# Moving the first sub-block's row moves ahead of a weight load, that load's cast to VectorE, and two pairs of band builds two units earlier, and dropping a gate on `w_out`

## The chip, the cores and the metric

The kernel runs on one core of one Trainium2 chip. The metric is device time in microseconds (us) of that core for one execution; lower is better. A run "of the same rounds" is a run of the kernel before that was taken on the same chip, in turn with the kernel it is compared with.

## The reference

A dynamic convolution over seven positions (weights from a softmax) feeds a feed-forward layer with squared ReLU:

```python
w = exp(weight_gen - max); w = w / sum(w)                # 8 x 4096 x 8 heads x 7
out = einsum('bshk,bskhg->bshg', w, windows of padded x) # x: 8 x 4096 x 192
x = out.reshape(32768, 192)
h = maximum(x @ w_in, 0)                                 # w_in: 192 x 2048
return h * h @ w_out                                     # w_out: 2048 x 192
```

## The kernel before

The work is cut into 64 sub-blocks of 512 tokens; blocks 0 and 1 have one sub-block, all others two. In each block, TensorE does three kinds of work. The convolution is a multiplication of x with band matrices. The *units* multiply with `w_in` (16 of them in a block of two sub-blocks; ScalarE applies the ReLU and VectorE squares, giving `g`). The *output matmuls* multiply `g` with `w_out`.

The convolution needs bands, which VectorE builds from the softmax weights. In the first sub-blocks, the rows of these weights are moved from one place in SBUF to another by small DMAs ("row moves", tile `wr`):

```python
def st_band(j, tiles):            # cut: one multiplication of moved rows with a mask
    nc.vector.tensor_tensor(out=bd_t[j][...], in0=wr_t[j][...], in1=mask[...], op=AluOp.mult)
```

The start of the program, with cuts:

```python
spin(25)                                  # warm-up matmuls on zeros
s0.load(nc.sync); s1.load(nc.sync)        # weight_gen of the first two parts
load_w_in(w_st[0], 0, nc.sync)            # first half of w_in, 768 KB as float32
x_load_f32(0)
load_w_in(w_st[1], 1, nc.sync)            # second half
# ... softmax of s0 and s1: exp on ScalarE, the rest on VectorE ...
nc.scalar.copy(out=w_i[:, 0, 0], in_=w_st[0])
wr_load_sbuf(0, [s0], range(NT), (nc.gpsimd,))   # row moves, sub-block 0
wr_load_sbuf(1, [s0], range(NT), (nc.sync,))
x_cast(0, nc.scalar.copy)
cross_w_in_by_pe(0)     # other partition half of w_in, first half: through TensorE
spin(14)
x_load_f32(1)
nc.scalar.copy(out=w_i[:, 1, 0], in_=w_st[1])
cross_w_in(1)           # the same for the second half: two 192 KB DMAs ("crossed copy")
# ... row moves of sub-blocks 2 and 3 ...
for i in range(NT):
    st_band(0, (i,))
st_conv(0)
nc.gpsimd.tensor_copy(out=gate, in_=x_st[1][:, 0:1])  # GpSimd waits for x here
for q in range(4):
    load_w_out(q, 4)
```

The output matmuls of most blocks use two PSUM banks, each with half of the contraction. ScalarE copies the first bank, then VectorE adds the second one, and only then is the pair free for the next output matmuls:

```python
def o_sum(j, qt, ccs, o):
    ...
    nc.scalar.copy(out=o_sb, in_=o[0][:, c])
    if len(o) == 2:
        nc.vector.tensor_tensor(out=o_sb, in0=o[1][:, c], in1=o_sb, op=AluOp.add)
```

A table places the bands of the next block at two units of the current one. Block 5 is made of sub-blocks 8 and 9, so block 4 builds their bands:

```python
us = {4: (10, 12), 6: (7, 9)}.get(j, (5, 9) if small else (1, 5))
for n, u in enumerate(us):
    at(j, u, "B", a + n)
```

The softmax here doesn't subtract the row's maximum and nothing guards it: scores larger than these inputs give would overflow.

Of the kernel before, what the change touches and what calls it, by code (L numbers as in the profile page):

```python
# [9 lines left out]
def kernel(  # L10
# [26 lines left out]
    nc = tc.nc  # L37
    f32 = mybir.dt.float32
# [9 lines left out]
    P = 128  # L48
# [13 lines left out]
    NT = 5  # L62
# [9 lines left out]
    const = ctx.enter_context(tc.tile_pool(name="const", bufs=1))  # L72
# [17 lines left out]
    w_i = const.tile([P, WQ, 2, NQ + NQ // 2], f16, name="w_i")  # L90
# [32 lines left out]
    x_st = {}  # L123

    def load_w_in(dst, q, eng):
        c = q * NQ
        eng.dma_start(out=dst[:, 0:NQ], in_=moe_w_in[0:P, c : c + NQ])  # L127
        for r0 in (0, RT):
            eng.dma_start(  # L129
                out=dst[r0 : r0 + RT, NQ:], in_=moe_w_in[P:D, c : c + NQ // 2]  # L130
            )
            c += NQ // 2

    def cross_w_in(q):
        for r0, r1 in ((0, RT), (RT, 0)):
            nc.sync.dma_start(out=w_i[r0 : r0 + RT, q, 1], in_=w_i[r1 : r1 + RT, q, 0])
# [144 lines left out]
    def tile_start(j, i):  # L281

        t1 = (j % NBB + 1) * TB
        return TB - P if i == NT - 1 and t1 in ends(j // NBB) else starts[i]
# [21 lines left out]
    def x_load_f32(j):  # L306
        x_st[j] = p_one.tile([P, (R + HALO) * HK], f32, name="x_st", tag="ex")
        block_load(
            j, x_st[j][:, 0 : NT * D].rearrange("p (t d) -> p t d", t=NT), x[j // NBB], D, nc.sync
        )  # L310

    def x_cast(j, copy):
        x_t[j] = p_x.tile([P, NT, D], f16, name="xt")
        copy(out=x_t[j].rearrange("p t d -> p (t d)"), in_=x_st[j][:, 0 : NT * D])
# [6 lines left out]
    def wr_load_sbuf(j, parts, order, engines):  # L321

        wr_t[j] = p_wr.tile([P, NT, HP, SL * 2], f16, name="wr")
        n = 0
        for i in order:
            t0 = max(j % NBB * TB + tile_start(j, i), 0)
            for s in parts:
                a, b = max(t0, s.t0), min(t0 + P, s.t0 + P * s.r)
                if a < b:
                    engines[n % len(engines)].dma_start(  # L330
                        out=wr_t[j][a - t0 : b - t0, i].rearrange("p g c -> p (g c)"),
                        in_=s.v[
                            (a - s.t0) // s.r : (b - s.t0) // s.r, HALO : HALO + s.r
                        ].rearrange("p r g c e -> p r (g c e)"),
                    )
                    n += 1

    def st_band(j, tiles):


        if j not in bd_t:
            bd_t[j] = p_bd.tile([P, H * NT * STEP], f16, name="bd")
        i = tiles[0]
        lo = STEP * i
        shift = 0 if i == 0 and j % NBB == 0 else lo - tile_start(j, i)
        n = min(STEP, P - shift)
        shape = (P, HP * len(tiles), n // SL, 2 * SL)
        nc.vector.tensor_tensor(  # L348
            out=bd_t[j][:, H * lo : H * (lo + len(tiles) * n)].rearrange(
                "p (g m c) -> p g m c", g=shape[1], c=2 * SL  # L350
            ),
            in0=wr_t[j][:, i : tiles[-1] + 1]
            .rearrange("p t g c -> p (t g) c")
            .unsqueeze(2)
            .broadcast_to(shape),
            in1=mask[:, shift : shift + n]
            .rearrange("p (m c) e -> p m (c e)", c=SL)
            .unsqueeze(1)
            .broadcast_to(shape),
            op=AluOp.mult,  # L360
        )
# [8 lines left out]
    def conv_pieces(j):  # L370


        s0, n = BLOCKS[j]
        th = n * TB // 2
        halves = []
        for half in (0, 1):
            s, a = (s0 + half, 0) if n == 2 else (s0, th * half)
            halves.append([
                (s, i, half, max(bounds[i], a), min(bounds[i + 1], a + th), a)
                for i in range(NT) if bounds[i] < a + th and bounds[i + 1] > a  # L380
            ])
        if n == 2:
            for k in range(NK):
                for later in (True, False):
                    for pair in zip(*halves):
                        for s, i, half, a, b, base in pair:
                            for q in (2 * k, 2 * k + 1):
                                yield later, s, i, q, half, a, b, base
        else:
            for pair in zip(*halves):  # L390
                for later in (True, False):
                    for k in range(NK):
                        for s, i, half, a, b, base in pair:
                            for q in (2 * k, 2 * k + 1):
                                yield later, s, i, q, half, a, b, base

    def st_conv(j):

        n = BLOCKS[j][1]
        th = n * TB // 2  # L400
        per = 1024 // th
        y = p_y.tile([P, NK, TB], f16, name="y")
        y_t[j] = y
        yps = [
            ps_h.tile([P, 2 * TB], f32, name="yp", tag="h") for _ in range(-(-NK // per))
        ]
        for later, s, i, q, half, a, b, base in conv_pieces(j):
            lo = bounds[i]
            hi = lo + (STEP if tile_start(s, i) == starts[i] else bounds[i + 1] - lo)
            _, ha, hb, pre = quads[q]  # L410
            m, h = (32, hb) if later else (pre, ha)
            bd = bd_t[s][:, H * lo : H * hi].rearrange("p (g c e) -> p g e c", g=HP, e=2)
            p0 = RT * half + 32 * (q % 2)
            k = q // 2
            col = th * (k % per) - base
            nc.tensor.matmul(  # L416
                out=yps[k // per][p0 : p0 + m, col + a : col + b],
                lhsT=x_t[s][:, i, 32 * q : 32 * q + m],
                rhs=bd[:, h // 2, h % 2, a - lo : b - lo],
                start=True,  # L420
                stop=True,
                skip_group_check=True,
                tile_position=(0, p0),
            )
        for n, yp in enumerate(yps):
            k0, k1 = n * per, min((n + 1) * per, NK)
            nc.scalar.copy(  # L427
                out=y[:, k0:k1, 0:th],
                in_=yp[:, 0 : (k1 - k0) * th].rearrange("p (k c) -> p k c", c=th),
            )  # L430
# [79 lines left out]
    with nc.allow_low_precision("fp16 matmul pipeline"), tc.manual_schedule():  # L510
# [16 lines left out]
                wr_load_sbuf(j, near, range(NT), engines)  # L527

        warm = const.tile([P, TB], f16, name="warm")
        gate = const.tile([P, 1], f32, name="gate")  # L530
        nc.vector.memset(warm, 0.0)  # L531
        for v in v_first:
            nc.vector.memset(v, 0.0)
# [3 lines left out]
        def spin(n):  # L537
# [3 lines left out]
        s0, s1, s2 = parts[:3]  # L541
# [6 lines left out]
        w_st = [  # L548
            p_wg.tile([P, (R + HALO) * HK], f32, name="w_st", tag="wg")[:, 0 : NQ + NQ // 2]
            for q in (0, 1)  # L550
        ]
        load_w_in(w_st[0], 0, nc.sync)
        x_load_f32(0)
        load_w_in(w_st[1], 1, nc.sync)
        for s in (s0, s1):
            s.exp(0, s.rh)
            s.total(0, s.rh)
            s.recip(0, s.rh)
            s.scale(0, s.rh, nc.vector)
        nc.scalar.copy(out=w_i[:, 0, 0], in_=w_st[0])  # L560
        wr_load_sbuf(0, [s0], range(NT), (nc.gpsimd,))
        wr_load_sbuf(1, [s0], range(NT), (nc.sync,))
        x_cast(0, nc.scalar.copy)
        cross_w_in_by_pe(0)
        spin(14)
        x_load_f32(1)
        nc.scalar.copy(out=w_i[:, 1, 0], in_=w_st[1])
        cross_w_in(1)
        wr_load_sbuf(2, [s0, s1], range(NT), (nc.gpsimd,))
        wr_load_sbuf(3, [s0, s1], range(NT), (nc.sync,))  # L570
        for i in range(NT):
            st_band(0, (i,))
        st_conv(0)

        nc.gpsimd.tensor_copy(out=gate, in_=x_st[1][:, 0:1])
        for q in range(4):
            load_w_out(q, 4)
        s2.load(nc.gpsimd)
# [18 lines left out]
        def at(j, u, kind, *args):  # L597
            fill.setdefault((j, u), []).append((kind, *args))
# [34 lines left out]
        for j in range(len(plans), NBLK - 1):  # L633
            a = BLOCKS[j + 1][0]
            small = [p for p in parts if p.fb <= j + 1][-1].r == FIRST
            us = {4: (10, 12), 6: (7, 9)}.get(j, (5, 9) if small else (1, 5))
            for n, u in enumerate(us):
                at(j, u, "B", a + n)
        for j in range(len(plans), NBLK):
# [86 lines left out]
        j = NBLK - 1  # L726
# [44 lines left out]
```

## Time and profile before

| | us |
|---|---|
| median of three runs | 750.5 (750.27 to 751.14) |
| span of the profiled run | 749.5 |
| TensorE busy | 739.9 |
| first convolution starts | 16.45 |
| first unit starts | 18.41 |
| crossed copy has landed | 19.0 |
| first output matmuls start | 24.56 |
| conv of block 5, start to start with the next work | 2.43 (1.53 for block 4's) |

Lines of the timeline have the start, the length, the engine, the line in the source, the operation, the tiles as out<-in, the shapes and the count. A bracket at the end gives the idle time of that engine just before, and what ended it. A group of several instructions may contain short gaps. TensorE is the bound throughout (busy 739.9 of 749.5 us): a change gains only by shortening the few stretches in which TensorE stands. The prediction shows the profile lines and reads them.

### The profile page before, as it was taken

To read this page: it belongs to the slowest core of one execution; us is meant where nothing else is said; L and a number is where in the kernel's file an instruction comes from. 1 tells how busy PE (TensorE), PEld (TensorE's weight loads), DVE (VectorE), ACT (ScalarE), POOL (GpSimd) and SP (SyncE) were. 2 spreads that over 40 slices of the span, in tenths; PEclk is the share of its full clock that TensorE was granted. 3 is DMA by queue.
4 is the path that set the end of the run, shared out by engine and by line. 5 is a ranking of instruction groups with operands and counts; after the bars stand their busy time and mean duration, and the time that the engine had idled before them with its cause. 6 is when DMAs were issued, how large, how long until landed. Compare 5 with 4: busy or idle time off the path is not lost.

```text
span 749.5 us, 33282 instructions
## 1 busy us (share of the span) xinstructions
PE 739.9 (99%) x15106; PEld 567.9 (76%) x15106; DVE 622.4 (83%) x1001; ACT 624.3 (83%) x755; POOL 89.4 (12%) x129
## 2 busy tenths in 40 slices
PE   7999999999999999999999999999999999999998
PEld 3867778877887777777877887787777777777787
DVE  6898898998889888888888888898888987677853
ACT  4998978888888888888888888888888887888883
POOL 7222220001101000011000110001100011000000
PEclk9999999999999999999999999999999999999999
DMA  7745444445453244543245442365441354342312
GB/s 216 117 97 117 79 67 114 99 76 138 94 116 64 76 73 80 128 90 66 45 80 138 87 80 53 51 138 108 59 80 46 58 108 80 59 72 52 50 45 65
DMA packets 122398, 64.81 MB, mean 86 GB/s; under 512 B 84107, under 2 KB 118865, under 8 KB 121745
## 3 DMA queue, kind: packets, MB, share of 16 engines
q1 hardware_dynamic: 77969, 45.69, 22.5%
q0 software_dynamic: 44144, 16.90, 20.1%
q8 instruction: 118, 1.93, 1.0%
q14 instruction: 23, 0.19, 0.1%
q10 hardware_dynamic: 144, 0.10, 0.0%
HBM read 48.61 MB, written 28.70 MB: 103 GB/s over the span
## 4 chain that ended last, share of the span: by engine, by line
PE 95%; DVE 2%; ACT 1%; DMA 1%; issue 0%; SPq 0%; ACTq 0%; DVEq 0%
PE o L475 45%; PE h L441 44%; PE yp L416 6%; DMA w_st<-in_moe_w_in_dram 1%; DVE bd L348 1%; DVE g L453 1%; ACT t L450 1%; PE wp L539 1%; DVE o_sb L491 0%; ACT w_i L560 0%; ACT y L427 0%; PE pt L144 0%; SPq L195 0%; SPq L129 0%; SPq L127 0%
## 5 line engine op out<-in xcount | busy, mean ns | idle before, releaser
L450 ACT ACTIVATE t<-h 128x1024 f16<-128x1024 f32 x512 | 496.7, 1027 | 66.7 <-PE h L441 66.1
L453 DVE TENSOR_TENSOR g<-t 128x1024 f16<-128x1024 f16 x512 | 335.5, 689 | 104.9 <-ACT t L450 102.7
L475 PEld LDWEIGHTS <-g 64*128 64x128 f16 (+1 forms) x8032 | 355.5, 94 | 51.7 <-issue 5.2
L475 PE MATMUL o<-w_o,g 64*128 64x192 f16 (+1 forms) x8032 | 387.3, 243 | 0.7 <-issue 0.5
L441 PE MATMUL h<-y,w_i 64*128 64x512 f16 (+1 forms) x3168 | 380.7, 370 | 1.4 <-ACT y L427 1.0
L441 PEld LDWEIGHTS <-w_i 64*128 64x128 f16 x3168 | 172.4, 94 | 108.2 <-issue 3.8
L348 DVE TENSOR_TENSOR bd<-wr,mask 128x4160 f16<-128x4160 f16 (+3 forms) x89 | 149.4, 1703 | 2.4 <-DMA wr<-v_first 2.3
L300 POOL DMA_DIRECT2D xt<-in_x_dram x62 | 51.7, 836 | 434.2 <-PE yp L416 411.1
L489 ACT COPY o_sb<-o 128x384 f32<-128x384 f32 x129 | 62.3, 483 | 32.9 <-PE o L475 32.9
L491 DVE TENSOR_TENSOR o_sb<-o,o_sb 128x384 f32<-128x384 f32 x123 | 68.4, 556 | 7.8 <-ACT o_sb L489 5.6
L427 ACT CAST y<-yp 128x1024 f16<-128x1024 f32 (+1 forms) x64 | 48.1, 802 | 15.9 <-PE yp L416 15.8
L416 PE MATMUL yp<-bd,xt 128*32 128x104 f16 (+8 forms) x3864 | 51.5, 208 | 0.6 <-DVE bd L348 0.4
L416 PEld LDWEIGHTS <-xt 128*32 128x32 f16 (+3 forms) x3864 | 46.0, 92 | 7.0 <-issue 6.7
L217 ACT ACTIVATE ex<-wg 128x448 f32<-128x448 f32 (+2 forms) x44 | 27.1, 615 | 2.2 <-DMA wg<-in_weight_gen_dram 2.2
L239 DVE TENSOR_TENSOR v_big<-ex,rcp 128x112 f16<-128x112 f32 (+1 forms) x136 | 27.4, 265 | 1.6 <-DMA vd<-v_big 0.4
L224 DVE TENSOR_REDUCE ssum<-ex 128x64 f32<-128x448 f32 (+2 forms) x44 | 26.2, 596 | 2.4 <-ACT ex L217 2.4
L231 DVE RECIPROCAL rcp<-ssum 128x64 f32<-128x64 f32 (+2 forms) x44 | 23.7, 539 | 1.5
L330 POOL DMA_DIRECT2D wr<-v_first x30 | 16.3, 562 | 34.4 <-DVE v_first L239 33.2
L290 POOL DMA_DIRECT2D xt<-in_x_dram x7 | 3.8, 549 | 133.1 <-PE yp L416 133.1
L539 PE MATMUL wp<-warm 128*128 128x512 f16 x39 | 12.3, 488 | 1.3 <-DVE warm L531 1.3
L539 PEld LDWEIGHTS <-warm 128*128 128x128 f16 x39 | 4.6, 119 | 8.3 <-issue 4.7
L239 DVE TENSOR_TENSOR v_first<-ex,rcp 128x112 f16<-128x112 f32 (+1 forms) x48 | 9.1, 257 | 0.3
(24 smaller groups left out, 29.1 us busy)
## 6 DMA issues: line engine op xcount, KB each, us to landing
out_dram<-o_sb SPq DMA_DIRECT2D x63, 384.0 KB, 2.9
xt<-in_x_dram POOLq DMA_DIRECT2D x42, 240.0 KB, 6.2
wg<-in_weight_gen_dram SPq DMA_DIRECT2D x4, 1064.0 KB, 7.9
xt<-in_x_dram POOLq DMA_DIRECT2D x20, 192.0 KB, 5.5
wr<-vd SPq DMA_DIRECT2D x38, 80.0 KB, 3.7
vd<-v_big SPq DMA_DIRECT2D x5, 512.0 KB, 5.7
wg<-in_weight_gen_dram SPq DMA_DIRECT2D x5, 392.0 KB, 5.2
wg<-in_weight_gen_dram SPq DMA_DIRECT2D x3, 616.0 KB, 5.2
```

The costliest lines, as they stand in the source:

```text
L217: nc.scalar.activation(out=self.ex[:, lo:hi].rearrange("p r g k e -> p (r g) k e"), in_=self.wg[:, lo:hi].rearrange("p r (g e) k -> p (r g ...
L239: eng.tensor_tensor(out=bass.AP(tensor=v.tensor, offset=v.offset + lo * H * SL + lo % SL * 2 + g * SL * 2, ap=[list(v.ap[0]), [H * SL + 2, ...
L300: eng.dma_start(out=dst[:, first:last], in_=ap)
L348: nc.vector.tensor_tensor(out=bd_t[j][:, H * lo : H * (lo + len(tiles) * n)].rearrange("p (g m c) -> p g m c", g=shape[1], c=2 * SL), in0= ...
L416: nc.tensor.matmul(out=yps[k // per][p0 : p0 + m, col + a : col + b], lhsT=x_t[s][:, i, 32 * q : 32 * q + m], rhs=bd[:, h // 2, h % 2, a - ...
L427: nc.scalar.copy(out=y[:, k0:k1, 0:th], in_=yp[:, 0 : (k1 - k0) * th].rearrange("p (k c) -> p k c", c=th),)
L441: nc.tensor.matmul(out=h[:, half, jj * th : (jj + 1) * th], lhsT=w_in_chunk(u * per + jj, slot, half), rhs=y_t[j][r0 : r0 + RT, k, 0:th], ...
L450: nc.scalar.activation(out=t1, in_=h, func=ActF.Relu)
L453: nc.vector.tensor_tensor(out=g, in0=t1, in1=t1, op=AluOp.mult)
L475: nc.tensor.matmul(out=oo[:, cc * Dm : (cc + 1) * Dm], lhsT=g[r0 : r0 + n, cc * P : (cc + 1) * P], rhs=w_o[r0 : r0 + n, fc, :], start=(fc ...
L489: nc.scalar.copy(out=o_sb, in_=o[0][:, c])
L491: nc.vector.tensor_tensor(out=o_sb, in0=o[1][:, c], in1=o_sb, op=AluOp.add)
```

## The change

The intent has three parts. The row moves of sub-block 0 are issued ahead of the second half of `w_in`, so that the first bands come earlier; in before that half was issued from 4.56 us and the moves from 8.63 us, and VectorE's wait for the moves ended at 13.90 us, 0.2 us after ScalarE's wait for the half. That half is then late and VectorE casts it, since it would follow the bands anyway. `w_out` no longer waits behind a GpSimd copy that reads x (1.13 us, after a wait of 1.55 us for that x). Far from the start, the bands for block 5 are placed two units earlier, so its convolution need not wait for them.

```diff
-        gate = const.tile([P, 1], f32, name="gate")
 ...
         load_w_in(w_st[0], 0, nc.sync)
         x_load_f32(0)
-        load_w_in(w_st[1], 1, nc.sync)
 ...
         nc.scalar.copy(out=w_i[:, 0, 0], in_=w_st[0])
-        wr_load_sbuf(0, [s0], range(NT), (nc.gpsimd,))
-        wr_load_sbuf(1, [s0], range(NT), (nc.sync,))
+
+        wr_load_sbuf(0, [s0], range(NT), (nc.sync, nc.gpsimd, nc.sync, nc.gpsimd, nc.gpsimd))
+        load_w_in(w_st[1], 1, nc.sync)
+        wr_load_sbuf(1, [s0], range(NT), (nc.gpsimd,))
         x_cast(0, nc.scalar.copy)
         cross_w_in_by_pe(0)
         spin(14)
         x_load_f32(1)
-        nc.scalar.copy(out=w_i[:, 1, 0], in_=w_st[1])
-        cross_w_in(1)
         wr_load_sbuf(2, [s0, s1], range(NT), (nc.gpsimd,))
-        wr_load_sbuf(3, [s0, s1], range(NT), (nc.sync,))
         for i in range(NT):
             st_band(0, (i,))
+        nc.vector.tensor_copy(out=w_i[:, 1, 0], in_=w_st[1])
+        cross_w_in(1)
+        wr_load_sbuf(3, [s0, s1], range(NT), (nc.sync,))
         st_conv(0)
-
-        nc.gpsimd.tensor_copy(out=gate, in_=x_st[1][:, 0:1])
         for q in range(4):
 ...
-            us = {4: (10, 12), 6: (7, 9)}.get(j, (5, 9) if small else (1, 5))
+            us = {4: (8, 10), 6: (7, 9)}.get(j, (5, 9) if small else (1, 5))
```

## The prediction

> **What bounds the kernel now.** I read the page first: busy shares, then the chain that ended last.
>
> ```profile
> PE 739.9 (99%) x15106; PEld 567.9 (76%) x15106; DVE 622.4 (83%) x1001; ACT 624.3 (83%) x755; POOL 89.4 (12%) x129
> ...
> PE 95%; DVE 2%; ACT 1%; DMA 1%; issue 0%; SPq 0%; ACTq 0%; DVEq 0%
> ```
>
> TensorE is busy 739.9 of 749.5 us and is 95% of the chain. So whatever the change does can act on the time in two ways only: it removes or adds time in which TensorE stands, or it does nothing. There are about 10 us in which TensorE stands, and all three parts of the change together can win a share of those. Next I read the chain in order of time for the first 20 us, because two of the three parts act there.
>
> ```profile
> 9.49 1.48 ACT w_i L560
> ...
> 11.82 4.71 PE wp L539 x14
> 16.52 1.02 PE yp L416 x55
> ```
>
> Columns: start, length, what. After the cast of the first w_in half, the chain runs through the 14 warm-up matmuls (L539) and then into the first convolution (L416), which starts at 16.5 us. The timeline of the same stretch shows what else is ready at 16.5 us:
>
> ```profile
> 8.63 4.45 POOL L330 DMA_DIRECT2D wr<-v_first  x8 [1.64 <-DVE v_first L239]
> ...
> 10.12 1.46 DVE L239 TENSOR_TENSOR v_first<-ex,rcp 128x112 f16<-128x112 f32 x8
> ...
> 13.68 1.47 ACT L567 CAST w_i<-w_st 128x1536 f16<-128x1536 f32 x1 [0.43 <-DMA w_st<-in_moe_w_in_dram]
> 13.90 4.87 DVE L348 TENSOR_TENSOR bd<-wr,mask 128x832 f16<-128x832 f16 x7 [2.32 <-DMA wr<-v_first]
> ```
>
> The row moves are issued from 8.63 us, but VectorE stands 2.32 us until the first of them has landed, at 13.90 us, 5.2 us after its issue (the view of tile wr gives 1.9 / 4.2 / 5.2 us from issue to landing as least, median and most). The second w_in half ends ScalarE's wait at 13.68 us, 0.2 us before. So the small moves landed right behind that 768 KB load (one 512 KB and two 128 KB issues). Five bands of one sub-block then take 13.90 to 16.50 us (0.50 us apart). **Two things are therefore ready at the same moment: the bands at 16.50 and the warm-up matmuls at 16.52.** Removing one alone frees nothing. The clock by stretches shows how long the warm-up lasts and why:
>
> ```profile
> 8.48:11.90 3.42, 1.10 (x6) 0.41 (x5) 3.03 (x10) 2.41 (x3) 3.27 (x6) 1.00 1.03 303
> 11.90:15.31 3.41, 3.41 (x10) 1.17 (x9) 1.41 (x3) 2.82 (x3) 2.41 (x6) 0.50 0.51 100
> ```
>
> First columns: stretch, length, TensorE busy; then weight loads, VectorE, ScalarE and GpSimd; the last three are granted clock, DMA share and GB/s. TensorE was busy 1.10 of 3.42 us (it stood 2.31 us for the first w_in half), and in the next stretch its clock was 0.50. DMA was full (1.03) until 11.9 us.
>
> Far from the start I looked for places where TensorE stands. The timeline of VectorE and of TensorE around 91 to 105 us, block 4, shows the largest:
>
> ```profile
> 93.56 0.69 DVE L453 TENSOR_TENSOR g<-t 128x1024 f16<-128x1024 f16 x1 [0.22 <-ACT t L450]
> 94.17 0.55 DVE L491 TENSOR_TENSOR o_sb<-o,o_sb 128x384 f32<-128x384 f32 x1
> 94.64 2.38 DVE L348 TENSOR_TENSOR bd<-wr,mask 128x832 f16<-128x832 f16 x2
> ...
> 98.14 2.35 DVE L348 TENSOR_TENSOR bd<-wr,mask 128x3328 f16<-128x3328 f16 x2
> ```
>
> ```profile
> 94.59 1.66 PE L475 MATMUL o<-w_o,g 64*128 64x192 f16 x32
> ...
> 100.08 1.86 PE L416 MATMUL yp<-bd,xt 128*32 128x104 f16 x118 [0.41 <-DVE bd L348]
> ```
>
> The convolution of block 5 begins at 99.44 and waits for its second pair of bands (ends 100.50). Start to start it takes 99.44 to 101.87 = 2.43 us, against 76.64 to 78.17 = 1.53 us for the one before: 0.90 us lost. The output matmuls at 102.53 take 1.55 instead of 1.33 us, waiting for a late sum on VectorE: 0.22 us more.
>
> [...]
>
> **The change, part by part.**
>
> *Moves ahead of the second half.* The moves of sub-block 0 now stand behind the first half and x only (ScalarE starts to cast that x at 10.87). Estimate from the least landing times of the same tile (1.9 to 2.8 us): issued 8.63 to about 10.4, landed by about 11 to 12.7. VectorE finishes both softmaxes at 11.58. So its bands run 11.6 to about 14.2 (5 x 0.50 plus a tail) instead of 13.9 to 16.5: **2.3 us earlier**. What that gives depends on the warm-up, whose count the diff leaves at 14:
> - Clock at 0.50 as in this profile: warm-up still ends at 16.5. Gain 0.
> - Clock full: 14 matmuls take 14 x 0.217 = 3.0 us from 11.65, so they end at 14.7. Before, bands hid that; now the convolution starts at 14.7. Gain 1.8 us.
>
> [...] I give the full clock 55%. Expected gain 1.0 us.
>
> *The second half later, cast by VectorE.* It is issued about 10.1 to 11.9 instead of 4.56 to 6.5. DMA engines then have only it, so I estimate landing at 14.5 to 15. The cast of 1536 columns is about 1.41 us (VectorE's 960-column cast, L314, took 0.88; x 1.6), and ends near 16.3; sub-block 1's bands (2.35) end near 18.7 and the cast of x near 19.6, as now (19.57). The crossed copy leaves at 16.3 instead of 15.2 and lands 3.3 to 3.8 us later (median 3.3), by 20.1. The first unit that needs it starts about 22.2 (20.4 in the fast case). Off the path, with little margin in the fast case. ScalarE loses a 1.47 us cast after which it stood idle anyway (2.4 us until L427): nothing.
>
> *w_out not held back.* Without the gate copy (1.13 us and a 1.55 us wait for x) GpSimd goes on after its moves. It has 14 of them now instead of 11, at about 0.55 us, so they end near 16.3 and w_out starts 2.0 us earlier (18.30 now). No TensorE wait for w_out is in the list of waits, so alone it gives nothing; in the fast case it is needed, since the first output matmuls move up to about 22.8 us.
>
> *Bands of block 5 at units 8 and 10.* The 0.90 and 0.22 us above should go. But VectorE keeps program order, and the first pair now stands before the g of units 8 and 9 and before the sum at 94.17, which frees the second output bank. The pair costs 96.94 - 94.64 = 2.30 us start to start. It can start at 92.53; the two g follow at 94.83 and 95.43 (0.60 each), the sum at 96.03, and ends near 96.58 instead of 94.72. The slack used up is 0.43 us. The output matmuls at 94.59 need that bank (they are already 0.11 us longer than 1.33), so **TensorE stands 1.87 us at 94.7**. Net: 1.87 - 0.90 - 0.22 = +0.75 us. TensorE is the bound from there to the end, so this stays.
>
> Sum: 750.5 - 1.0 + 0.75 = 750.25, taken as 750.2.
>
> **Rivals.**
> - *Full gain at the start in every run* (the warm-up no longer holds): for it, the two ends differed by 0.02 us only. Against it, the warm-up is unchanged and stands in the chain. Then 749.4.
> - *Half clock in most runs:* nothing won at the start, 751.25.
> - *The new stand at 94.7 trips the clock.* [...] I give it 10%.
> - *The output bank does not hold TensorE:* the last change alone gains 1.1 us. Against it, the matmul at 94.59 already waits for this very sum. Then 748.4 to 749.4.
> - *The second half is late:* TensorE waits at unit 4 for the crossed copy, up to 1 us. Slack about 2 us in the slow case speaks against it.
>
> **Range and chances.** The two states of the clock give 749.4 and 751.25; widened for the tripped clock above and the absent bank wait below: 748.6 to 752.2. 2% is 15 us, more than all TensorE stands, so within 2% 0.98, faster 0.01, slower 0.01.
>
> **What would show it.** In the changed profile: first bands at about 11.6 with no wait for a move; the first convolution starting the moment L539 ends, 14.7 or 16.5; the L314 and w_in casts on VectorE done by about 19.6; w_out issues from about 16.3; at block 4 the sum (L491) ending near 96.6 after the band pair, and TensorE standing near 1.9 us in L475 there, while the convolution of block 5 no longer waits. The prediction is wrong if TensorE does not stand there, or if the convolution at the start waits on something else than the warm-up.

The sum came to 750.5 - 1.0 + 0.75 = 750.25 us, taken as 750.2. Its -1.0 is 55% of 1.8 us. The 1.8 us is 16.5 - 14.7, with 0.217 us for one warm-up matmul at full clock; in before, 15 weight loads of the first warm-up span 3.12 us from 5.08 us at a granted clock of 1.00, which is 14 steps of 0.216 us and a load of 0.10. That VectorE keeps program order can be read in block 4 of before (sum 94.17, bands 94.64 us) and of the changed kernel (bands 92.29, sum 95.80 us).

## The result, and the profile after

| kernel | median us | lowest to highest | runs |
|---|---|---|---|
| before | 750.38 | 750.1 to 751.14 | 4 |
| after | 750.8 | 750.18 to 751.94 | 4 |

The ratio after over before is 1.0006, with a 95% interval of 0.9988 to 1.0023. All outputs are right. 0.0006 of 750.4 is 0.45 us. The two cannot be told apart by time.

The page of the changed kernel: busy time by engine, and the shares of the chain that ended last.

```profile
PE 738.3 (99%) x15106; PEld 558.1 (75%) x15106; DVE 623.0 (83%) x1002; ACT 623.1 (83%) x754; POOL 90.7 (12%) x131
...
PE 93%; DVE 3%; DMA 2%; ACT 1%; issue 0%; SPq 0%; DVEq 0%; ACTq 0%
```

TensorE still has all the same instructions and is busy 738.3 of 748.5 us. Its share of the chain has fallen from 95% to 93%, and VectorE and DMA have each gained a point. That is no measure of the change: from 118.16 to 132.11 us the chain of this profile runs over VectorE, ScalarE and one DMA of 5.26 us, while the list of TensorE's waits has none there. The span is 1.0 us shorter than in the profile of before. This must not be read as a gain: much later in the program TensorE has small pauses without any wait shown (0.31 us at 193.84 us in the profile of before), which differ from run to run. So I compare landmarks up to 120 us instead, where all of the change acts.

The start, in the timeline of the changed kernel (the warm-up has line L538 here, L539 before; the cast of the second half is L570):

```profile
8.36 1.29 SPq L330 DMA_DIRECT2D wr<-v_first  x2
...
11.50 2.09 DVE L348 TENSOR_TENSOR bd<-wr,mask 128x832 f16<-128x832 f16 x4
...
14.60 0.59 DVE L348 TENSOR_TENSOR bd<-wr,mask 128x832 f16<-128x832 f16 x1 [1.01 <-DMA wr<-v_first]
15.85 0.96 DVE L570 CAST w_i<-w_st 128x1536 f16<-128x1536 f32 x1 [0.65 <-DMA w_st<-in_moe_w_in_dram]
...
12.21 3.18 PE L538 MATMUL wp<-warm 128*128 128x512 f16 x14
15.32 0.90 PE L416 MATMUL yp<-bd,xt 128*32 128x104 f16 x72
...
17.43 3.28 POOL L161 DMA_DIRECT2D w_o<-in_moe_w_out_dram  x4
```

Four bands start at 11.50 us with no wait, 2.4 us earlier than before. The fifth waits until 14.60 us for its row move. The warm-up runs at full clock this time (granted 1.00 from 12.20 to 15.40 us): 3.18 us, against 4.87 before (granted 0.50 from 11.90 to 15.31 us). The first convolution starts at 15.32 us, 1.13 us earlier, at the moment the warm-up ends. Then the cost shows, in the copy's issue and on TensorE:

```profile
16.83 1.52 SPq L136 DMA_DIRECT2D w_i<-w_i  x2
...
20.95 0.38 PE L441 MATMUL h<-y,w_i 64*128 64x256 f16 x3
22.25 2.03 PE L441 MATMUL h<-y,w_i 64*128 64x256 f16 x33 [0.92 <-DMA w_i<-w_i]
```

The crossed copy is issued at 16.83 us, lands at 22.2 us, and TensorE stands 0.92 us for it. Of the 1.23 us by which the first unit was early, 0.34 us are left after this, at the second group of units (25.64 us against 25.98).

In block 4, TensorE and then VectorE:

```profile
94.35 0.24 PE L475 MATMUL o<-w_o,g 64*128 64x192 f16 x1
96.40 1.48 PE L475 MATMUL o<-w_o,g 64*128 64x192 f16 x31 [1.80 <-DVE o_sb L491]
...
101.07 1.57 PE L416 MATMUL yp<-bd,xt 128*32 128x104 f16 x120
...
92.29 2.38 DVE L348 TENSOR_TENSOR bd<-wr,mask 128x832 f16<-128x832 f16 x2
94.59 1.29 DVE L453 TENSOR_TENSOR g<-t 128x1024 f16<-128x1024 f16 x2
95.80 0.55 DVE L491 TENSOR_TENSOR o_sb<-o,o_sb 128x384 f32<-128x384 f32 x1
```

The pair of bands at 92.29 us now stands ahead of two `g` and of the sum at 95.80 us (94.17 before). The second output matmul needs the bank that this sum frees, and TensorE stands 1.80 us. The convolution behind it (101.07 us) no longer waits. The granted clock was 1.00 from 90 to 103 us.

| position on TensorE, relative to before (us) | start of it in before | after |
|---|---|---|
| first unit | 18.41 | -1.23 |
| second group of units | 25.98 | -0.34 |
| output matmuls ahead of the stand | 91.98 | -0.24 |
| units behind the stand | 96.03 | +1.62 |
| units behind the conv and its output matmuls | 104.73 | +0.47 |
| later in block 5 | 119.84 | +0.40 |

So the two parts cancel: 0.34 us won and still 0.24 us of it there at block 4, then 1.86 us lost at the stand and 1.15 us returned by the conv and the sum behind it, a net loss of 0.71 us. Together they give +0.40 us.

### The profile page after: what moved, and what is told of

The parts are those of the page before. It is cut to its first block, busy times and chain, and to the rows that moved or that the text cites. A ratio compares the mean times of both kernels' runs of the same rounds, so it can differ in the third digit from the quotient of the medians.

```text
span 748.5 us, 33278 instructions
## 1 busy us (share of the span) xinstructions
PE 738.3 (99%) x15106; PEld 558.1 (75%) x15106; DVE 623.0 (83%) x1002; ACT 623.1 (83%) x754; POOL 90.7 (12%) x131
## 3 DMA queue, kind: packets, MB, share of 16 engines
q1 hardware_dynamic: 77537, 45.64, 22.3%
## 4 chain that ended last, share of the span: by engine, by line
PE 93%; DVE 3%; DMA 2%; ACT 1%; issue 0%; SPq 0%; DVEq 0%; ACTq 0%
PE o L475 44%; PE h L441 43%; PE yp L416 6%; DVE g L453 1%; DMA vd<-v_big 1%; DMA w_st<-in_moe_w_in_dram 1%; DMA w_i<-w_i 1%; DVE bd L348 1%; DMA wg<-in_weight_gen_dram 0%; ACT t L450 0%; DVE o_sb L491 0%; DVE v_big L239 0%; DVE v_first L239 0%; DVE ssum L224 0%; DVE rcp L231 0%
## 5 line engine op out<-in xcount | busy, mean ns | idle before, releaser
L441 PEld LDWEIGHTS <-w_i 64*128 64x128 f16 x3168 | 164.5, 94 | 114.8 <-issue 3.2
L416 PE MATMUL yp<-bd,xt 128*32 128x104 f16 (+7 forms) x3864 | 51.0, 208 | 0.1
L330 POOL DMA_DIRECT2D wr<-v_first x33 | 18.4, 578 | 33.9 <-DVE v_first L239 32.9
L538 PE MATMUL wp<-warm 128*128 128x512 f16 x39 | 11.7, 469 | 1.3 <-DVE warm L530 1.3
L538 PEld LDWEIGHTS <-warm 128*128 128x128 f16 x39 | 4.5, 117 | 7.8 <-issue 3.8
```

Source lines behind the costliest of these rows:

```text
L416: nc.tensor.matmul(out=yps[k // per][p0 : p0 + m, col + a : col + b], lhsT=x_t[s][:, i, 32 * q : 32 * q + m], rhs=bd[:, h // 2, h % 2, a - ...
L441: nc.tensor.matmul(out=h[:, half, jj * th : (jj + 1) * th], lhsT=w_in_chunk(u * per + jj, slot, half), rhs=y_t[j][r0 : r0 + RT, k, 0:th], ...
```

## The experiments

The theory after the result: (a) the band placement costs about 0.7 us, because it delays a sum which frees a PSUM bank; (b) the start gains little, because the crossed copy becomes the next wait. Its rivals: the loss lies in the clock state of one run, `w_out` delays the copy, or the softmax work ahead makes VectorE late at block 4. Each profile shows one execution, which can lie at the edge of its kernel's times; where that matters, it is said.

### Bands alone

Before, with `(10, 12)` -> `(8, 10)` as the only edit.

> The kernel before, with the bands of block 5 at units 8 and 10 and nothing else. Theory (the sum on VectorE now stands behind the first band pair, so the output bank comes free late): TensorE stands 1.8 to 2.0 us in the output matmuls near 94.6 us, the convolution of block 5 no longer waits (0.9 us won), the output matmuls after it neither (0.2 us won): 0.6 to 0.8 us later than before from about 105 us on. Rival (placing the bands sooner only removes waits, and the stand at 94.6 in the changed kernel came from the changed start): no stand there, 1.1 us earlier than before.

Measured: 751.89 us (6 runs) against 751.16 (11 runs), ratio 1.0013 (1.0001 to 1.0026). TensorE in block 4:

```profile
97.93 1.48 PE L475 MATMUL o<-w_o,g 64*128 64x192 f16 x31 [1.81 <-DVE o_sb L491]
```

The stand is 1.81 us, the net loss between the landmarks at 91.98 and 104.73 us is 0.72 us. Part (a) is confirmed, in a kernel whose start is untouched. In the 3.41 us around this stand TensorE was busy 1.60 us, and the clock stayed at 1.00.

### Start alone

The changed kernel, with `(8, 10)` back to `(10, 12)`.

> The changed kernel, with the bands of block 5 back at units 10 and 12. Theory: at the output matmuls near 24 us it is 0.2 to 0.5 us ahead of before if the clock is full in the warm-up, because TensorE waits about 1 us for the crossed copy of the second half at unit 4; if the clock is at half there, the convolution starts at 16.4 to 16.6, that wait is gone, and it is 0 to 0.1 us ahead. No stand near 94.6; the 0.9 us wait in the convolution of block 5 is back. Time 0.3 us under before, 0.8 us under the changed kernel. Rival (the crossed copy's wait in the changed profile was a chance of one run): no wait at unit 4 and 1.2 us ahead at full clock.

Measured: 750.62 us (6) against 751.16 (11), ratio 0.9991 (0.9978 to 1.0003). In the first convolution, TensorE:

```profile
15.44 0.44 PE L416 MATMUL yp<-bd,xt 128*32 128x96 f16 x22 [0.34 <-DVE bd L348]
```

The stand in block 4 is gone and the convolution waits 0.41 us for a band again. The profiled run is at full clock (warm-up 3.18 us) and 0.90 us ahead at 26 us, more than expected; it is the fastest of the six (748.62 us, the others 750.55 to 751.64). The waits are spread: 0.34 us for the fifth band, 0.40 for the cast of x, 0.13 for the crossed copy (landed 21.3 us) and 0.18 for `w_out`. So the copy is one of several events that lie close together, not the only one. A gain is possible but not shown.

### Start with the gate put back

The kernel of the previous run plus the line that the change removed:

```diff
+        nc.gpsimd.tensor_copy(out=gate, in_=x_st[1][:, 0:1])
         for q in range(4):
             load_w_out(q, 4)
```

> As e2_start_only, with the gate that holds w_out back until the second x has landed. Theory [...]: the copy lands in 3.3 to 4 us after its first issue instead of 5.4, TensorE waits under 0.3 us at unit 4 at full clock; w_out's last quarter lands after 28 us, and the second half of the first output matmuls (27.5 us) waits up to 1 us for it. Rival (the copy is late because its source is cast late, not because of w_out): the wait at unit 4 stays at 0.8 us or more.

Measured: 750.01 us (5) against 751.16 (11), ratio 0.9985 (0.9972 to 0.9997). `w_out` started at 18.90 us instead of 17.68, yet the copy landed at 22.27 us, 4.6 us after its second issue. That `w_out` is what delays the copy is therefore not confirmed. The profiled run fell in the half-clock warm-up (8 of its matmuls took 2.54 us from 14.40 us, where all 14 take 3.18 us at full clock; convolution at 16.87 us), so TensorE came later and did not wait for the copy. This profile stands 0.33 us *behind* before at 26 us, so it gives no mechanism for the time. The interval lies only just below 1, in one of twelve experiments, and I do not take it as a gain.

### Both band pairs at unit 10

Before, with `(10, 12)` -> `(10, 10)`.

> The kernel before, with both band pairs of block 5 at unit 10, behind the sum that frees the output bank. Theory: no stand at 94.6 (at most 0.15 us, as before), both pairs done by about 99.4, the convolution waits at most 0.2 us: 0.9 to 1.1 us earlier than before from about 105 us on. Rival (VectorE is so full there that the later squares or sums hold TensorE instead): a wait of 0.5 us or more appears in the output matmuls behind the convolution, and nothing is won.

Measured: 751.54 us (5) against 751.16 (11), ratio 1.0006 (0.9994 to 1.0018). TensorE:

```profile
99.92 1.60 PE L416 MATMUL yp<-bd,xt 128*32 128x104 f16 x120
...
103.30 1.48 PE L475 MATMUL o<-w_o,g 64*128 64x192 f16 x31 [0.95 <-DVE o_sb L491]
```

The convolution no longer waits, but the output matmuls behind it do: 0.95 us for a sum that VectorE reached late. The rival is right: from the sum at 94.65 us to the one at 102.70 us VectorE has no gap in this run. In such a stretch a new order only chooses who waits.

### The fifth move on SyncE's queue

The start-alone kernel, with the fifth engine in the list of the first row moves `nc.gpsimd` -> `nc.sync`, so that three moves stand on SyncE ahead of the load.

> As e2_start_only, with the fifth row move of sub-block 0 on SyncE too, so that all moves of SyncE and GpSimd for that sub-block are issued before the second w_in half. Theory (in the changed kernel the third GpSimd move, issued at 9.85, lands at 14.5 [...]): the fifth band starts by 13.6 with no wait over 0.2 us and the bands end by about 14.2; the second half is issued 0.6 us later, so the crossed copy lands 0.3 to 0.8 us later and the wait at unit 4 grows. Rival (GpSimd's moves are slow by themselves): no change for the tile that GpSimd moves last.

(The theory tested here was that the load makes the move late.)

Measured: 753.62 us (4) against 750.87 (9), ratio 1.0039 (1.0018 to 1.006). VectorE, then TensorE, then the clock by stretches (columns as in the prediction):

```profile
11.93 2.59 DVE L348 TENSOR_TENSOR bd<-wr,mask 128x832 f16<-128x832 f16 x5
17.46 0.96 DVE L570 CAST w_i<-w_st 128x1536 f16<-128x1536 f32 x1 [2.93 <-DMA w_st<-in_moe_w_in_dram]
...
21.50 0.91 PE L416 MATMUL yp<-bd,xt 128*32 128x104 f16 x72 [2.70 <-DVE xt L314]
25.05 3.80 PE L441 MATMUL h<-y,w_i 64*128 64x256 f16 x33 [1.27 <-DMA w_i<-w_i]
...
20.50:24.00 3.50, 1.40 (x75) 0.97 (x75) 3.50 (x7) 0.94 (x2) 3.10 (x5) 1.00 1.36 227
24.00:27.40 3.40, 2.35 (x24) 1.70 (x26) 2.10 (x2) 1.02 (x1) 0.13 (x1) 0.50 1.55 262
```

All five bands run without a wait and end at 14.52 us. This fits the theory that the fifth move of the changed kernel, issued on GpSimd at 9.85 us, just after the load began to be issued (9.69 us), landed late because of it. The two moves that GpSimd had issued ahead of the load were in time there (four bands ran from 11.50 us), so its queue is not slow by itself; but this run changed the queue and the order together. The price is everything else. VectorE waits 2.93 us for the load, its cast starts at 17.46 us (16.11 in the start-alone run), and the copy is now issued at 18.45 us, behind `w_out` (17.41 us). It lands at 25.00 us. TensorE waits 2.70 and 1.27 us, and another 0.87 between, and its clock falls to half (0.50) from 24.0 to 30.8 us. At 26 us this run is 5.2 us behind; it is the slowest of the four (755.90 us, the others 752.05 to 754.33), and its row moves started 0.4 us later than in the changed kernel. The second half of `w_in` has no slack left.

### `w_out` held until the copy has landed

The start-alone kernel, with a gate that reads the copy's output:

```diff
+        nc.gpsimd.tensor_copy(out=gate, in_=w_i[:, 1, 1, 0:1])
```

> As e2_start_only, with w_out held back until the crossed copy has landed (the gate reads it). Theory [...]: the copy lands 3.3 to 3.7 us after its first issue, by 20.8, no wait at unit 4 in either state of the clock; w_out starts near 22, lands near 31, and TensorE waits 2 us or more in the second half of the first output matmuls. Rival (the copy takes 4.2 to 5.4 us by itself): it lands as late as in the three runs of this start so far (21.3 to 22.3).

Measured: 756.71 us (4) against 750.87 (9), ratio 1.0082 (1.0056 to 1.0108). The copy landed at 21.45 us, 3.7 us after its second issue, without any `w_out` beside it; in before it took 3.3 us, in the changed kernel 4.8. Counted from its first issue at 17.21 us, as in the expectation, it took 4.2 us. This and the landing lie inside what the rival had said (4.2 to 5.4 us, 21.3 to 22.3 us), and the copy was no faster than in two runs with `w_out` beside it (3.7 us in start alone, 3.6 in softmax later with the bands as in before). So the rival held. The first output matmuls then stand:

```profile
28.96 2.50 PE L475 MATMUL o<-w_o,g 128*128 128x192 f16 x16 [4.43 <-DMA w_o<-in_moe_w_out_dram]
```

`w_out` was issued at 22.09 us and landed from 28.92 us on. So the gate in before was harmless only because it opened at 18.30 us.

### Softmax work later, bands as in before

The start-alone kernel, with a piece of softmax of a later part moved out of block 4: `(1, 2): ((4, 6), (5, 1), (5, 15))` -> `((5, 1), (5, 6), (5, 15))`, and the load to fit.

> As e2_start_only (bands at 10 and 12), with one piece of softmax on VectorE (2.1 us) moved from unit 6 of block 4 to block 5. Theory (VectorE has no slack between 84 and 105 us, so any order of the same work there makes TensorE wait somewhere): with 2.1 us less of it, the bands end before the convolution and the sum behind it is in time, so both waits (0.9 and 0.2 us) go: 1.0 to 1.2 us ahead of e2_start_only at 112 us. Rival (it only moves the wait into block 5): a wait of similar size appears between 104 and 128 us.

Measured: 752.36 us (5) against 750.87 (9), ratio 1.0027 (1.0013 to 1.0041). TensorE, then VectorE ahead of its bands:

```profile
99.33 1.88 PE L416 MATMUL yp<-bd,xt 128*32 128x104 f16 x118 [0.41 <-DVE bd L348]
119.40 1.48 PE L475 MATMUL o<-w_o,g 64*128 64x192 f16 x31 [1.38 <-DVE o_sb L491]
...
91.90 0.69 DVE L453 TENSOR_TENSOR g<-t 128x1024 f16<-128x1024 f16 x1 [1.01 <-ACT t L450]
```

The wait of the convolution is still 0.41 us. VectorE is free earlier, but then it stands 1.01 us for ScalarE: the bands come behind `g` and a sum which depend on TensorE itself, and these are no earlier. The moved work causes a new stand of 1.38 us in block 5. The rival was right.

### Softmax work later, bands at 8 and 10

The changed kernel with the same move of softmax work.

> The changed kernel, bands at 8 and 10, with the same softmax piece moved to block 5. Theory: the stand of TensorE near 94.6 us comes from VectorE's order and shrinks by the slack that the moved piece gives, less what VectorE then waits for ScalarE: 0.6 to 1.1 us instead of 1.8 to 1.9. Rival (the stand comes from something else, such as the landing of row moves): it stays at 1.8 us.

Measured: 751.82 us (4) against 750.87 (9), ratio 1.0013 (0.9999 to 1.0026). TensorE:

```profile
96.24 1.48 PE L475 MATMUL o<-w_o,g 64*128 64x192 f16 x31 [0.83 <-DVE o_sb L491]
```

Here the theory held: the stand falls from 1.80 to 0.83 us, since with the early bands VectorE really had been late. But a stand of 1.00 us appears at the same place of block 5. Nothing is won. At the start this run also shows the clock falling to half from 16.96 to 20.37 us (48 matmuls of a unit group take 4.36 us from 17.12 us, against 2.80 in the changed kernel), after TensorE had waited 1.04 us for the fifth band and 0.89 us for y.

### One band pair on GpSimd

Before with `(8, 10)`, and the bands of sub-block 8 built by GpSimd, which has little to do there (in before it issues four row moves from 87.39 us and then stands until 102.22 us):

```diff
+        eng = nc.gpsimd if j == 8 else nc.vector
-        nc.vector.tensor_tensor(
+        eng.tensor_tensor(
```

> The kernel before, bands of block 5 at units 8 and 10, the first pair (sub-block 8) made by GpSimd, which stands there. Theory (the stand at 94.6 is VectorE's order, and the later waits are VectorE's load): no stand at 94.6, no wait in the convolution of block 5 if GpSimd ends by 99.4 [...], no late sum behind it: 1.0 to 1.2 us ahead at 112 us of where the run is at 91 us. Rivals: GpSimd takes over 8 us and the convolution waits for it; or VectorE is slowed while GpSimd reads the same memory, and its sums come late again.

Measured: 758.65 us (4) against 750.87 (11), ratio 1.0107 (1.0087 to 1.0126). GpSimd, VectorE and TensorE:

```profile
89.93 8.20 POOL L350 TENSOR_TENSOR bd<-wr,mask 128x832 f16<-128x832 f16 x2
91.00 7.82 DVE L239 TENSOR_TENSOR v_big<-ex,rcp 128x112 f16<-128x112 f32 x4
101.76 2.71 PE L477 MATMUL o<-w_o,g 64*128 64x192 f16 x31 [6.49 <-DVE o_sb L493]
```

The pair takes 8.20 us instead of 2.38, and four softmax multiplications on VectorE beside it take 7.82 us instead of 0.83. TensorE stands 6.49 us and runs at half clock (0.50) from 99.37 to 106.2 us. Why the two are slow beside each other, and how long the pair takes on GpSimd alone, no run shows.

### The start with the gate, and the GpSimd band

The changed kernel with the gate of the third experiment and the band on GpSimd.

> The changed kernel with the hold-back of w_out kept, and the first band pair of block 5 on GpSimd: the best start and the best block 4. Theory: as e9_gpsimd_band at block 4, and at the start as e3_hold_back: 1.2 to 2.0 us under before. Rival as for e9_gpsimd_band.

Measured: 758.04 us (4) against 750.87 (11), ratio 1.0094 (1.0078 to 1.011). It failed in the same way (the pair takes 8.20 us on GpSimd, TensorE stands 6.48 us). Its start shows the half clock from 10.81 to 17.64 us (the warm-up takes 5.44 us), and it was 1.97 us behind at 26 us, although the crossed copy landed only 3.2 us after its second issue.

### The changed kernel again

No edit; this run was for the spread of the start and of the stand.

> The changed kernel once more, for a second look at its start and a ratio from the same rounds. Theory: the stand at 94.6 is 1.8 to 1.9 us again and block 4 costs 0.6 to 0.8 us in sum, as in any run; the start differs from run to run between 0.9 us ahead and 0.6 us behind the first profile of before, with the landing of the first w_in half and the clock; ratio 0.999 to 1.001. Rival (the start gives about the same each time): 0.3 to 0.4 us ahead again at 26 us.

Measured: 751.66 us (6) against 750.87 (11), ratio 1.0013 (0.9996 to 1.0029).

```profile
23.55 2.03 PE L441 MATMUL h<-y,w_i 64*128 64x256 f16 x33 [0.93 <-DMA w_i<-w_i]
...
98.16 1.48 PE L475 MATMUL o<-w_o,g 64*128 64x192 f16 x31 [1.80 <-DVE o_sb L491]
```

The stand in block 4 repeats to the hundredth, and the net loss there is 0.73 us. The start does not repeat. This time the warm-up is at half clock and TensorE still waits 0.93 us for the copy, which took 5.6 us from its second issue and landed at 23.50 us. At 26 us the run is 0.95 us behind before; it is the slowest of the six.

### One bank for two output quarters

Before with `(8, 10)`, and the third and fourth quarter of block 3's outputs, which are computed in the course of block 4, in one bank each, so that no VectorE sum stands between them:

```diff
-                    o = new_o(ps_o, 1, qt % 2) if j < 2 else new_o(ps_o)
+                    one = j < 2 or (j == 3 and qt >= 2)
+                    o = new_o(ps_o, 1, qt % 2) if one else new_o(ps_o)
```

> The kernel before, bands of block 5 at units 8 and 10, and the last two quarters of block 3 (their output matmuls run in block 4) summed in one bank with 128 rows, as blocks 0 and 1 are, so that ScalarE alone copies them out and VectorE has no sum to do there (0.55 us less, twice). Theory: with no sum on VectorE behind the bands, the output matmuls near 94.6 do not wait, the convolution of block 5 does not wait, nor do the output matmuls behind it: 1.1 to 1.2 us of waits gone, at the cost of 4 times 0.05 to 0.12 us for the 128-row form: 0.6 to 1.0 us ahead at 112 us of where the run is at 91 us. Rival (ScalarE's copy or the squares now come late instead): under 0.3 us ahead.

Measured: 749.47 us (6) against 750.73 (11), ratio 0.9988 (0.9974 to 1.0002). TensorE and VectorE:

```profile
95.15 1.49 PE L475 MATMUL o<-w_o,g 128*128 128x192 f16 x16
100.05 1.58 PE L416 MATMUL yp<-bd,xt 128*32 128x104 f16 x120
...
92.50 2.39 DVE L348 TENSOR_TENSOR bd<-wr,mask 128x832 f16<-128x832 f16 x2
94.81 1.29 DVE L453 TENSOR_TENSOR g<-t 128x1024 f16<-128x1024 f16 x2
96.01 2.36 DVE L348 TENSOR_TENSOR bd<-wr,mask 128x3328 f16<-128x3328 f16 x2
```

The bands stand where the change put them, but neither the stand nor the wait of the convolution is there. What made the early placement costly was the sum behind it: without that sum, no wait is left in block 4. The one-bank form costs some 0.1 us per group (1.42 us start to start at 95.15 us, against 1.32 for the two-bank group at 102.22 us), and two of its four groups run before the landmark at 91.98 us; so the net is taken from the output matmuls at 85.35 us, ahead of all four. From there to 119.84 us the run gains 0.58 us. The time leans the same way, but its interval contains 1.

## Why the prediction was right or wrong

The measured 750.8 us lies in the range and within 2%, as predicted, and 0.6 us above the predicted 750.2. The time says little about the working: 2% is 15 us and the kernel had only some 10 us to win, and neither the predicted -0.25 us nor the measured +0.45 us can be told from nothing in an interval of -0.9 to +1.7 us. For the case of the profile, the full clock, the prediction had 749.4; that its average of two cases came nearer is luck. (The range was also narrower than the prediction's own cases: 748.4 us for an absent bank wait lies outside it.) So the landmarks have to decide. Point by point:

**Bands 2.3 us earlier (11.6 to 14.2).** The first four began at 11.50 us without a wait, as predicted. The fifth ended at 15.19 us, 1.3 us earlier than before, because its move landed late, 14.60 us. The run with all moves ahead of the load agrees that the load held it.

**The convolution starts as the warm-up ends, at 14.7 or 16.5 us, depending on the clock.** Confirmed in these two: it started with the warm-up's end in the profile after (15.32 us, because the first half of `w_in` had come 0.55 us later) and in the repeat (16.61 us, half clock). In two other profiles of this start, start alone and softmax later with bands at 8 and 10, the warm-up ended earlier (convolution from 14.32 and 13.98 us), and the convolution then stood 0.34 and 1.04 us for the fifth band. That is the sign of being wrong that the prediction had named, so this point holds only where the warm-up ends late enough to hide the fifth band. Two profiles of kernels with the old start at full clock (both bands at unit 10, band on GpSimd) had the convolution at 15.2 and 15.1 us but the first unit at 18.56 and 18.43, as in before at half clock (18.41): there the bands hide the clock, as I had said.

**The second half is off the path, with little margin in the fast case: this is the step that failed.** My sum took the start as worth 1.0 us on average, 1.8 at full clock. At full clock the first unit was 1.23 us earlier, but 0.34 us remained at 26 us. Three of the sizes behind it were wrong. I had the half land at 14.5 to 15 us because "DMA engines then have only it", an estimate for which I gave no rate; VectorE's wait for it ended at 15.85 us, though it had been issued at about the predicted time. Row moves and 480 KB of x went out beside it, and the DMA share was 0.82 from 10.40 to 13.80 us and 0.93 in the 3.4 us after; that these held it up is my reading, which only the fifth move's run touches. The cast took 0.96 us, not 1.41: I had scaled a cast that was slower than the 0.66 us of the same cast in the profile after. And the crossed copy took 5.4 us from its first issue, not 3.8 (from its second 4.8, not 3.3), and landed at 22.2 us instead of 20.1: 0.5 us of this came from the later issue, 1.6 us from the copy itself. The rival "the second half is late" named this wait, with up to 1 us; 0.92 us came. I had discounted it by the slack of the slow case, and the repeat showed that even there it can wait 0.93 us.

How much the start is worth can be seen across the ten profiles whose start is that of before or of the change as it stands (those with a gate or another order are left out). The position at the second group of units, relative to before's profile:

| start as | profiled runs, full clock in the warm-up | half clock | mean |
|---|---|---|---|
| before | +0.15, +0.03 | 0.00, +0.90, -0.14 | +0.19 |
| changed | -0.34, -0.90, -0.75, +0.58 | +0.95 | -0.09 |

The difference of the means, 0.3 us, is far below the spread of either row, so the mean gain is not measured: neither nothing nor the expected 1.0 us is excluded. What is shown is that at full clock all four profiles fall far short of the 1.8 us forecast for that case, and that waits for the crossed copy are in the profile in four of the five changed starts (0.92, 0.13, 0.46 and 0.93 us). Why the copy takes 3.1 to 3.3 us from its second issue with the old start (five profiles) and 3.2 to 6.0 us with the new one and its variants (nine) stays open: `w_out` beside it was not shown to be the cause, and with the gate of before it took 4.6 us once and 3.2 once. The order of the moves and the cast on VectorE were not tested apart.

The prediction gave the full clock 55%, an estimate of mine that no trace or run supports. What the traces show: in all fourteen profiles the clock of this warm-up goes with the time that TensorE stood just before it, for the first half of `w_in`. After 0.71 to 1.91 us (seven profiles) the warm-up took 3.18 us; after 2.10 to 3.69 us (the other seven) it took 4.87 us or more. No run changed that stand on purpose, so this is a regularity and not a tested cause. Nor does it give a threshold: stretches in which TensorE was busy 1.10 of 3.42 us (before, from 8.48 us), 1.40 of 3.50 (all moves ahead of the load, from 20.50 us) and 1.69 of 3.46 (softmax later, bands at 8 and 10, from 13.50 us) were followed by the half clock, but 2.24 of 3.40 (changed kernel, from 10.40 us) and 1.60 of 3.40 (changed kernel, from 94.00 us) were not.

**`w_out` alone gives nothing.** It was issued at 17.43 us instead of 18.30 (predicted 16.3). Even so TensorE waited 0.18 us for it in the start-alone run and 0.27 us in the one with the softmax work later. So a later issue would probably cost time in the fast case (no run with a gate had the full clock in the new start), and in the run with the longest hold it cost 4.43 us.

**Bands of block 5: a stand of 1.87 us and a net loss of 0.75.** Confirmed to a few hundredths: 1.80 us and 0.71 net, 0.72 with the bands alone, 0.73 in the repeat.

**The stand does not trip the clock (10% that it does).** It did not, in three profiles: the granted clock was 1.00 from 94 to 104 us in the changed kernel, from 94.79 to 98.20 us with the bands alone and from 96.0 to 99.4 us in the repeat.

So the sum -1.0 + 0.75 became -0.34 + 0.71, plus 0.03 of drift between: the mis-sized term is the gain at the start, 0.34 us instead of 1.8 in this full-clock profile. The end of the span cannot check this to better than about 1 us, for the reason given with the result.

## What to carry to other kernels

When two or three things become ready at nearly the same time, removing one of them gains only up to the next: read which wait is third and fourth in line, with its own landing time under the *new* traffic, before counting the gain. An instruction placed earlier can delay those behind it on its engine: here the band pair placed at 92.29 us put the two `g` at 94.59 us and the sum at 95.80 us, 1.63 us later than before. Ask which of those frees a buffer that the bounding engine needs, here that 0.55 us sum. Where an engine has no gap between two such needs, a new order only moves the wait. Moving other work off that stretch moved it too (1.38 and 1.00 us in block 5); taking two sums off the engine for good removed both waits here, though no run's time proves the gain.
